# The decays of three batches as exponentials of one scan over logarithms

## The chip, the core and the metric

The kernel runs on one core of a Trainium2 chip. The metric is device time in microseconds (us), the median of three runs. TensorE (PE), VectorE (DVE), ScalarE (ACT), GpSimd (POOL) and SyncE (SP, which issues the transfers) each work through a queue of their own and wait for one another through semaphores.

## What is computed

```python
# B, H, S, D = 4, 8, 768, 48;  f_logit = randn * 0.5 + 2
f = 1.0 / (1.0 + np.exp(-f_logit))
for t in range(S):
    state = f[:, :, t, :, None] * state + np.einsum('bhd,bhe->bhde', k[:, :, t], v[:, :, t])
    y[:, :, t] = np.einsum('bhd,bhde->bhe', q[:, :, t], state)
x = y.transpose(0, 2, 1, 3).reshape(B, S, H * D)
h = x.transpose(0, 2, 1) @ U @ V            # over the sequence, rank 32
u = x + h.transpose(0, 2, 1)
out = u + np.maximum(u @ w_ch1, 0.0) @ w_ch2   # 384 -> 1536 -> 384
```

A gated linear attention and behind it a mixer. The weights U, V, w_ch1 and w_ch2 come in 64 bits and are converted in the kernel.

## The kernel before

**Units and chunks.** The attention is cut into 16 units n: batch b = n // 4 and a pair of its heads, whose channels lie in the two halves of the 128 partitions. The 768 time steps are 12 chunks of C = 64. Inside a chunk a query meets a key by a product q·k (scores, masked to be causal), and between chunks a state of 48 x 48 per head is carried. For that each key is multiplied by X, the product of the gates behind it to the end of its chunk, and each query by Y, the inverse of that product; `least` is the factor of a whole chunk, and `whole` that factor without its first chunk, spread over 48 columns for the scan of the states (L1051). `prepare(n)` holds the steps up to the operands, `attend(n)` those on the operands: `kept` turns the scaled keys `kz` back on TensorE (L1002), `states` makes `ds` (L1026), `scan` adds up the states (L1051, copied to `st` by GpSimd at L1057 in batches 1 and 2), `scores` and `mask` (L975, L988), `read` (L1069) and `inner` (L1087) give y.

**Gates before.** Batch 0 (n < 4) has logarithms of the gates summed by a product on TensorE with a triangle of ones (`log_sums`), and all its factors are exponentials. Batches 1 to 3 work with the gates themselves. `gates` brings raw f to a tile with time along the row and takes its sigmoid into `fz`: units 4 and 5 (n < TURNED = 6) are turned by six transposes on TensorE (L777, `on_tensor`) into one of three PSUM tiles of 4 KB per partition, from unit 6 on VectorE turns them (L754). The raw tiles are `late[:, 0:3]` for even n and `other[:, 0:3]` for odd n. `keep` scans the gates backward into X (L876), copies `least` (L881), and makes `starts` by a maximum and a reciprocal (L883, L884) and `whole` (L886). `keys` multiplies k by X (L802, or L805 behind a transpose). `read` (in the order: read_back) scans the gates forward into Y from `starts` (L894), and `queries` multiplies q by Y.

**The order of work.** TensorE's queue is written by hand in the whole program. VectorE's and ScalarE's are written by hand through batch 0's mixer and the first third of batch 1; behind that a scheduler orders them, and it orders GpSimd throughout. The stretch around units 4 and 5 is this loop (L1286 on), where batch 0's first mixer products run (a tile `pz` of 12 matmuls at L300, emptied by a Relu on ScalarE at L335; two PSUM tiles are shared by `pz`, `pw` and `po`), then a piece of weight conversion is issued, then from the fourth turn on one step of the attention:

```python
second = chain(front(HP, "gates", "keep", "keys", "read_back", "queries"), steps(HP, 2 * HP + 1))
for i, (_, piece) in enumerate(start + m.firsts[1:]):
    piece()
    for f in loads[: 2 if i in (0, 2) else 1]:
        loads.remove(f)
        f()
    if i >= EARLY:
        next(second)()
```

A piece of conversion (`weight_loader`) is two passes on ScalarE (L91, L92), three on VectorE (L98 to L100) and an addition on GpSimd (L101). `w_y` and `w_r` are its tiles. Twelve pieces of w_ch1 are followed by twelve of w_ch2, which the mixer's second product (`po`, L355) reads. Behind the stretch the loop `attention` puts `fill()`, pieces of the mixer of the batch before, between the steps of the units, so that TensorE always has products of the mixer beside those of the attention.

Of the kernel before, what the change touches and what calls it, by code (L numbers as in the profile page):

```python
# [10 lines left out]
F32 = mybir.dt.float32  # L11
# [3 lines left out]
AF = mybir.ActivationFunctionType  # L15
# [549 lines left out]
def factored_path(ctx, tc, q, k, v, f_logit, moe_U, moe_V, moe_w_ch1, moe_w_ch2, out, ok):  # L565
# [135 lines left out]
    for s in range(2):  # L701
        half = causal[s * C : (s + 1) * C, :]
        nc.gpsimd.affine_select(out=half, in_=half, compare_op=ALU.is_ge, fill=0.0, base=0,
                                pattern=[[1, C]], channel_multiplier=-1)
    ends = late[:, 3, :]
    nc.vector.memset(ends, 0.0)
    nc.vector.memset(ends.rearrange("p (c t) -> p c t", t=C)[:, :, C - 1], 1.0)
    starts = other[:, 3, :]
    nc.vector.memset(starts, 0.0)
    fz = [const.tile([P, S + 1], F32, name=f"fz{i}") for i in range(2)]  # L710

    kz = [const.tile([P, C + S], F32, name=f"kz{i}") for i in range(2)]
    for i in range(2):
        nc.gpsimd.memset(kz[i][:, 0:C], 0.0)
    least = const.tile([P, NU, NCH], F32, name="least")

    wholes = [const.tile([P, NCH], F32, name=f"whole{i}") for i in range(2)]
    added = const.tile([P, D * NCH + 1], F32, name="added")
    nc.gpsimd.memset(added[:, 0:1], 0.0)
    for i in range(2):  # L720
        nc.gpsimd.memset(wholes[i][:, 0:1], 0.0)

    U = const.tile([P, NBL, R], F32, name="U")
    V = const.tile([P, (NBL * R + P - 1) // P, P], F32, name="V")
# [22 lines left out]
    def backwards(t, first, n):  # L747

        a = t[:, first : first + 1]
        return bass.AP(a.tensor, a.offset, [list(a.ap[0]), [-1, n]])  # L750

    def turned(t, src_tile):

        nc.vector.transpose(  # L754
            t.rearrange("p (c i) -> p c i", i=NB), src_tile.rearrange("p (c d) -> p c d", d=NB),
        )
# [3 lines left out]
    def prepare(n):  # L760
# [2 lines left out]
        T = units[n] = {}  # L763
        b = n // HP
        r, f = raw[n % 2], fz[n % 2]
        by_chunk = f[:, 0:S].rearrange("p (c t) -> p c t", t=C)

        def follow(nm):

            if n >= HP and n + 2 < NU:  # L770
                load(n + 2, nm)

        def on_tensor(nm):

            pt = ps_big.tile([P, 2, 512], F32, name="pt", tag="big")
            for c in range(NBL):
                nc.tensor.transpose(  # L777
                    pt[:, 2 * c // NBL, c % (NBL // 2) * P : (c % (NBL // 2) + 1) * P],
                    nat[n % 2][nm][:, c].rearrange("p h d -> p (h d)"), ident,
                )  # L780
# [59 lines left out]
        def keep_logs():  # L840
            def blocks_of(t):
                return t.rearrange("p (a c t) -> p a c t", a=2, t=P)

            T["X"], T["Y"] = late[:, 4 + n % 2, :], fz[n % 2][:, 0:S]
            of_least = least[:, n, :].rearrange("p (a c s) -> p a c s", a=2, s=2)
            if n == 0:
                parts = [(slice(a, a + 1), t) for a, t in enumerate(T["sums"])]
            else:
                parts = [(slice(0, 2), T["both"])]
            parts = [(a, t[:, :, 0 : NBL // 2 * (P + 2)].rearrange("p a (c t) -> p a c t", t=P + 2)) for a, t in parts]  # L850
            for a, sums in parts:
                nc.scalar.activation(blocks_of(T["X"])[:, a], sums[:, :, :, 0:P], AF.Exp, scale=-1.0)
            for a, sums in parts:
                nc.scalar.activation(blocks_of(T["Y"])[:, a], sums[:, :, :, 0:P], AF.Exp)
            for a, sums in parts:
                nc.scalar.activation(of_least[:, a], sums[:, :, :, P : P + 2], AF.Exp, scale=-1.0)
            nc.scalar.copy(wholes[n % 2][:, 1:NCH], least[:, n, 1:NCH])

        def gates():
            f0 = T["f0"] = two.tile([P, NCH], F32, name="f0")  # L860
            if n < TURNED:
                pt = on_tensor("f")
                nc.scalar.activation(halves(f)[:, :, :, 1:C], pt[:, :, :, 1:C], AF.Sigmoid)
                nc.scalar.activation(f0.rearrange("p (a c) -> p a c", a=2), pt[:, :, :, 0], AF.Sigmoid)
                follow("f")
                return
            fT = late[:, 6, :]
            turned(fT, r["f"])
            follow("f")
            fv = fT.rearrange("p (c t) -> p c t", t=C)  # L870
            nc.scalar.activation(by_chunk[:, :, 1:C], fv[:, :, 1:C], AF.Sigmoid)  # L871
            nc.scalar.activation(f0, fv[:, :, 0], AF.Sigmoid)

        def keep():
            X = T["X"] = late[:, 4, :]
            nc.vector.tensor_tensor_scan(  # L876
                backwards(X, S - 1, S), backwards(f, S, S), backwards(ends, S - 1, S), 0.0,
                ALU.mult, ALU.add,
            )
            X0 = X.rearrange("p (c t) -> p c t", t=C)[:, :, 0]  # L880
            nc.vector.tensor_copy(least[:, n, :], X0)  # L881
            X1 = two.tile([P, NCH], F32, name="X1")
            nc.vector.tensor_single_scalar(X1, X0, LEAST, ALU.max)  # L883
            nc.vector.reciprocal(starts.rearrange("p (c t) -> p c t", t=C)[:, :, 0], X1)  # L884
            whole = wholes[n % 2]
            nc.vector.tensor_tensor(whole[:, 1:NCH], T["f0"][:, 1:NCH], X0[:, 1:NCH], ALU.mult)  # L886

        def keys():
            operand("k", "X")
# [1 line left out]

        def read():
            Y = T["Y"] = late[:, 5, :]
            nc.vector.tensor_tensor_scan(Y, f[:, 0:S], starts, 0.0, ALU.mult, ALU.add)  # L894

        def queries():
            operand("q", "Y")
# [59 lines left out]
    def attend(n):  # L957
# [50 lines left out]
                spread()  # L1008

        def spread():  # L1010
            whole = T["whole"] = one.tile([P, D, NCH], F32, name="whole")
            nc.scalar.copy(whole, wholes[n % 2].unsqueeze(1).broadcast_to((P, D, NCH)))

        def halves_of(n):
            return [slice(0, D // 2), slice(D // 2, D)] if n == HP - 1 else [slice(0, D)]
# [23 lines left out]
        def scan():  # L1039

            st = T["st"] = two.tile([P, NCH, D], F32, name="st")
            by_e = "p (e c) -> p c e"
            if b == 0:
                states = st.rearrange("p c e -> p (c e)")
                T["st"] = states.rearrange(by_e, c=NCH)
            else:
                states = added[:, 0 : D * NCH]
            with tc.high_priority(offset=2 * AHEAD):
                for e in halves_of(n):
                    of = slice(e.start * NCH, e.stop * NCH)  # L1050
                    nc.vector.tensor_tensor_scan(  # L1051
                        states[:, of], added[:, of], T["whole"].rearrange("p e c -> p (e c)")[:, of], 0.0, ALU.add, ALU.mult
                    )
                if b == B - 1:
                    nc.scalar.copy(st, states.rearrange(by_e, c=NCH))
                elif b:
                    nc.gpsimd.tensor_copy(st, states.rearrange(by_e, c=NCH))  # L1057
# [125 lines left out]
    with tc.manual_schedule(engines={nc.vector.engine, nc.scalar.engine}):  # L1183
# [511 lines left out]
```

## Time and profile before

| what | before |
|---|---|
| three runs | 466.26, 466.35, 466.47 us; median 466.35 |
| the profiled execution: from its first to its last instruction | 463.2 us; the page gives no time for it beside this span |
| TensorE busy | 455.2 us, 98% of the span; granted clock 0.999 |
| VectorE busy | 351.4 us, 76% |
| ScalarE busy | 170.4 us, 37% |
| GpSimd busy | 48.5 us, 10% |

In rows of the order of time the first number is the start in us from the span's start, the second the length; the bracket at the end holds the idle time of the engine before the instruction and what ended it. In groups stand the count, the busy time in us, the mean of one in ns and the idle time before. `out<-in` names the tiles, then come their shapes as partitions x elements. L876 is line 876 of the kernel before. In rows of the compiled order (below) a scan is called SCALAR_TENSOR_TENSOR, and `x6` stands for six equal instructions in a row.

### The profile page before, as it was taken

What the parts mean: (1) busy time and instruction counts of PE and PEld (TensorE: products, weight loads), DVE (VectorE), ACT (ScalarE), POOL (GpSimd) and SP (SyncE); (2) the same over time, 40 slices, a digit from 0 to 9 for tenths busy, and PEclk for the clock granted to TensorE, in tenths of its full rate; (3) what the DMA queues carried; (4) which work ended last, traced back from release to release, by engine and by line L of the source; (5) the groups of instructions that cost most, each with busy time, mean ns of one, the idle gap of its engine ahead of it and who ended that gap; (6) DMA issues with size and microseconds to landing.
All of it is one profiled execution on the core that took longest, in us unless ns stands there. A gap on an engine that the chain in (4) does not pass through costs nothing.

```text
span 463.2 us, 13016 instructions
## 1 busy us (share of the span) xinstructions
PE 455.2 (98%) x5639; PEld 394.5 (85%) x5639; DVE 351.4 (76%) x585; ACT 170.4 (37%) x323; POOL 48.5 (10%) x56
## 2 busy tenths in 40 slices
PE   8999999999999999999999999999999999999997
PEld 5886888875666578999898888899989999999996
DVE  6778788979999677676765559977797887858652
ACT  6785776562333143323322323451412311212200
POOL 2002445634112001010000000000000000000000
PEclk9999999999999999999999999999999999999999
DMA  9959997577777604504633030100000000000001
GB/s 194 186 139 212 227 217 180 150 119 103 124 113 118 107 18 53 78 1 89 77 52 74 14 61 4 28 3 21 18 1 1 35 1 23 13 1 35 1 36 39
DMA packets 148583, 34.35 MB, mean 74 GB/s; under 512 B 136934, under 2 KB 146982, under 8 KB 148518
## 3 DMA queue, kind: packets, MB, share of 16 engines
q1 hardware_dynamic: 147718, 33.29, 37.1%
q8 instruction: 46, 0.75, 0.7%
q10 hardware_dynamic: 800, 0.15, 0.2%
q14 instruction: 19, 0.16, 0.1%
HBM read 28.70 MB, written 4.72 MB: 72 GB/s over the span
## 4 chain that ended last, share of the span: by engine, by line
PE 80%; DVE 11%; ACT 3%; DMA 2%; issue 2%; SPq 2%; DVEq 0%; ACTq 0%
PE pw L389 27%; PE pz L300 21%; PE pp L495 12%; PE po L355 5%; PE y L1069 2%; PE sc L975 2%; PE ds L1026 2%; PE y L1087 2%; PE pt L1002 1%; SPq L661 1%; DVE late L894 1%; PE pt L777 1%; DVE late L876 1%; PE pt L835 1%; DMA other<-in_f_logit_dram 1%
## 5 line engine op out<-in xcount | busy, mean ns | idle before, releaser
L300 PE MATMUL pz<-uT,w 128*128 128x256 f32 x492 | 111.5, 382 | 0.3
L300 PEld LDWEIGHTS pz<-uT,w 128*128 128x128 f32 x492 | 91.7, 190 | 12.9 <-ACT uT L289 0.6
L389 PE MATMUL pw<-zw,w_raw 128*128 128x192 f32 x216 | 38.0, 329 | 0.0
L389 PE MATMUL pw<-w,z_all 128*128 128x192 f32 x216 | 37.3, 327 | 0.0
L335 ACT ACTIVATE z_all<-pz 128x512 f32<-128x512 f32 x33 | 19.6, 598 | 45.1 <-PE pz L300 44.7
L389 PEld LDWEIGHTS pw<-w,z_all 128*128 128x128 f32 x216 | 35.3, 190 | 0.5
L389 PEld LDWEIGHTS pw<-zw,w_raw 128*128 128x128 f32 x216 | 35.1, 190 | 0.6 <-issue 0.3
L101 POOL TENSOR_TENSOR w<-w_y,w_r 128x384 int32<-128x384 int32 x24 | 31.5, 1311 | 37.0 <-DVE w_y L100 22.5
L876 DVE TENSOR_TENSOR_SCAN late<-fz,late 128x768 f32<-128x768 f32 x12 | 21.1, 1755 | 9.4 <-ACT fz L871 9.3
L488 ACT ACTIVATE other<-other 128x512 f32<-128x512 f32 x18 | 11.3, 630 | 40.3 <-DVE other L204 40.3
L355 PE MATMUL po<-w,zw 128*128 128x384 f32 x72 | 25.2, 495 | 0.0
L355 PE MATMUL po<-w,z_all 128*128 128x384 f32 x72 | 24.7, 493 | 0.0
L1057 POOL COPY st<-added 128x576 f32<-128x576 f32 x8 | 12.4, 1556 | 113.8 <-DVE added L1051 113.8
L988 DVE TENSOR_TENSOR A<-sc,causal 128x768 f32<-128x768 f32 x16 | 15.2, 953 | 8.5 <-PE sc L975 8.5
L355 PEld LDWEIGHTS po<-w,zw 128*128 128x128 f32 x72 | 13.2, 190 | 9.6 <-issue 0.8
L894 DVE TENSOR_TENSOR_SCAN late<-fz,other 128x768 f32<-128x768 f32 x12 | 21.0, 1750 | 0.2
L355 PEld LDWEIGHTS po<-w,z_all 128*128 128x128 f32 x72 | 13.3, 190 | 8.9 <-DVE o L204 0.6
L488 ACT ACTIVATE z_all<-z_all 128x512 f32<-128x512 f32 x12 | 7.6, 631 | 34.1 <-DVE z_all L204 34.1
L1034 ACT COPY added<-ds 48x576 f32<-48x576 f32 (+2 forms) x29 | 17.8, 619 | 4.5 <-PE ds L1026 4.1
L495 PE MATMUL pp<-v_nat,late 128*128 128x128 f32 x152 | 19.1, 275 | 0.0
L1069 PEld LDWEIGHTS y<-st,qT 48*64 48x64 f32 x704 | 13.6, 137 | 6.2 <-issue 4.5
L98 DVE TENSOR_SCALAR w_y<-w_y 128x384 f32<-128x384 f32 (+3 forms) x27 | 12.1, 449 | 8.8 <-ACT w_y L91 8.8
(233 smaller groups left out, 872.1 us busy)
## 6 DMA issues: line engine op xcount, KB each, us to landing
w_raw<-in_moe_w_ch_dram SPq DMA_DIRECT2D x18, 384.0 KB, 3.6
out_dram<-o SPq DMA_DIRECT2D x17, 192.0 KB, 1.9
v_nat<-in_v_dram SPq DMA_DIRECT2D x16, 144.0 KB, 3.8
v_nat<-in_v_dram SPq DMA_DIRECT2D x32, 72.0 KB, 3.5
zw<-in_moe_w_ch_dram SPq DMA_DIRECT2D x6, 384.0 KB, 5.1
out_dram<-o SPq DMA_DIRECT2D x14, 96.0 KB, 2.2
w<-in_k_dram SPq DMA_DIRECT2D x4, 288.0 KB, 4.1
w<-in_q_dram SPq DMA_DIRECT2D x4, 288.0 KB, 4.2
```

Source lines behind the costliest of these rows:

```text
L101: nc.gpsimd.tensor_tensor(dst.bitcast(I32), shaped(y.bitcast(I32)), shaped(r), ALU.add)
L300: nc.tensor.matmul(pm[:, i * 2 * P : (i + 1) * 2 * P], lhsT=w1[:, m, o : o + P], rhs=uT[a][:, m, :], start=(m == 0), stop=(m == NDC - 1))
L335: nc.scalar.activation(z[a, c][:, k : k + 2, :].rearrange("p i t -> p (i t)"), pm, AF.Relu)
L355: nc.tensor.matmul(pm, lhsT=z[a, i // NI][:, i % NI, s * P : (s + 1) * P], rhs=w2[:, i, :], start=(i == 0), stop=(i == NFC - 1))
L389: nc.tensor.matmul(W["pm"][:, n * HM : (n + 1) * HM], lhsT=lhs[:, i, :], rhs=rhs[:, i, :], start=(i == 0), stop=(i == NI - 1))
L488: nc.scalar.activation(dst, dst, AF.Relu, scale=float(SIGNS[n]))
L495: nc.tensor.matmul(pm[:, i, r * P : (r + 1) * P], lhsT=room["w"](wn)[:, r * P : (r + 1) * P], rhs=x_node(a, xn), start=((xn, wn) == of[0]) ...
L876: nc.vector.tensor_tensor_scan(backwards(X, S - 1, S), backwards(f, S, S), backwards(ends, S - 1, S), 0.0, ALU.mult, ALU.add,)
L894: nc.vector.tensor_tensor_scan(Y, f[:, 0:S], starts, 0.0, ALU.mult, ALU.add)
L988: nc.vector.tensor_tensor(T["A"], sc[:, :, 0 : NBL * C].rearrange("p h (c i) -> p h c i", i=C), causal.unsqueeze(1).unsqueeze(1).broadcast ...
L1034: nc.scalar.copy(added[r, 1:].rearrange("p (e c s) -> p e c s", c=NBL, s=2)[:, e], ds[r, :, 0 : NBL * D].rearrange("p s (c e) -> p e c s", ...
L1069: nc.tensor.matmul(o(c % 2, par, c // 2), lhsT=T["q"][rows[par], chunk[c]], rhs=T["st"][rows[par], c, :], start=(c <= 2), stop=False, skip ...
```

## The change

Batches 1 to 3 get their factors from logarithms, too, without TensorE's product. `gates` first raises raw f to at least FLOOR = -40 in place, on VectorE for units 4 and 5 and on GpSimd from unit 6 on; then f is turned as before, and ScalarE makes exp(-f) and log(1 + exp(-f)), the negative logarithm of the gate, in `fz`. `keep` is one backward scan of these logarithms, which starts again at each chunk's end (`within` is 1, and 0 there), and behind it two exponentials on ScalarE: X for the first 63 columns of each chunk (the last column of `late[:, 4:6]` is set to 1 once), and `least`. `read` is one more exponential, of the same sums with the other sign, in place of the second scan. The copy, the maximum, the reciprocal and the product for `whole` fall away, and so do the sigmoids with `f0`; `whole` is one tile, filled from `least` directly, which drops a copy in batch 0's `keep_logs` as well. The tiles `ends` and `starts` go, and with them some memsets.

TensorE's queue keeps its 965 rows and their order. On VectorE, at unit 4, behind the ninth piece of weights; `late` holds the raw f of unit 4, X and the constants of the scan, `fz` the gates or their logarithms. Before:

```order
L98 TENSOR_SCALAR w_y<-w_y 128x384
L99 TENSOR_SCALAR w_y<-w_y 128x384
L100 SCALAR_TENSOR_TENSOR w_y<-w_raw,w_y 128x384
L876 SCALAR_TENSOR_TENSOR late<-fz_128,late 128x768
L881 COPY least<-late 128x12
L883 TENSOR_SCALAR X_1141<-late 128x12
L884 RECIPROCAL other<-X_1141 128x12
L886 TENSOR_TENSOR whole_135<-f_1107,late 128x11
```

and now:

```order
L98 TENSOR_SCALAR w_y<-w_y 128x384
L99 TENSOR_SCALAR w_y<-w_y 128x384
L100 SCALAR_TENSOR_TENSOR w_y<-w_raw,w_y 128x384
L859 TENSOR_SCALAR late<-late 128x12x48
L98 TENSOR_SCALAR w_y<-w_y 128x384
L99 TENSOR_SCALAR w_y<-w_y 128x384
L100 SCALAR_TENSOR_TENSOR w_y<-w_raw,w_y 128x384
L869 SCALAR_TENSOR_TENSOR fz_127<-late,fz_127 128x768
```

A new instruction of VectorE, the floor (L859 of the changed kernel), stands behind six pieces of weights and ahead of the seventh, and f's transposes on TensorE (L776 there) now wait for it; the four small steps behind the scan are gone. Unit 5 has the same one behind six more pieces. On GpSimd, around units 6 and 7 (`late` and `other` are their raw f, `w_90` is w_ch2), before:

```order
L101 TENSOR_TENSOR w_89<-w_y,w_r 128x3x128 x12
L101 TENSOR_TENSOR w_90<-w_y,w_r 128x384 x6
L1057 COPY st<-added 128x576
L101 TENSOR_TENSOR w_90<-w_y,w_r 128x384 x6
L1057 COPY st<-added 128x576 x7
```

and now:

```order
L101 TENSOR_TENSOR w_89<-w_y,w_r 128x3x128 x12
L101 TENSOR_TENSOR w_90<-w_y,w_r 128x384 x2
L859 TENSOR_SCALAR late<-late 128x768
L101 TENSOR_TENSOR w_90<-w_y,w_r 128x384 x4
L1044 COPY st<-added 128x576
L101 TENSOR_TENSOR w_90<-w_y,w_r 128x384 x4
L859 TENSOR_SCALAR other<-other 128x768
```

The additions of w_ch2's pieces now have the floors of units 6 and 7 between them. On VectorE around units 7 and 8, in the last third of batch 1 (`other` and `late` are the raw tiles, `o` is a result of the mixer), before:

```order
L884 RECIPROCAL other<-X_1725 128x12
L886 TENSOR_TENSOR whole_136<-f_1715,late 128x11
L754 STREAM_TRANSPOSE kz_131<-other 128x768
L805 TENSOR_TENSOR kz_131<-kz_131,late 128x768
L1051 SCALAR_TENSOR_TENSOR added<-added,whole 128x576
L204 TENSOR_TENSOR o<-x,po 128x384
L988 TENSOR_TENSOR A<-sc,causal 128x768
L894 SCALAR_TENSOR_TENSOR late<-fz_129,other 128x768
L754 STREAM_TRANSPOSE qT<-other 128x768
L805 TENSOR_TENSOR qT<-qT,late 128x768
L754 STREAM_TRANSPOSE late<-late 128x768
L876 SCALAR_TENSOR_TENSOR late<-fz_128,late 128x768
```

and now:

```order
L751 STREAM_TRANSPOSE fz_128<-other 128x768
L869 SCALAR_TENSOR_TENSOR fz_128<-late,fz_128 128x768
L751 STREAM_TRANSPOSE kz_130<-other 128x768
L804 TENSOR_TENSOR kz_130<-kz_130,late 128x768
L1038 SCALAR_TENSOR_TENSOR added<-added,whole 128x576
L204 TENSOR_TENSOR o<-x,po 128x384
L976 TENSOR_TENSOR A<-sc,causal 128x768
L751 STREAM_TRANSPOSE qT<-other 128x768
L804 TENSOR_TENSOR qT<-qT,late 128x768
L751 STREAM_TRANSPOSE fz_127<-late 128x768
L869 SCALAR_TENSOR_TENSOR fz_127<-late,fz_127 128x768
```

The scan of Y (L894) that stood between the mask and the transpose of q is gone, the scan of X (L869 now) writes the sums into `fz`, and the order of the others is kept. ScalarE has, for a unit, exp and log in place of a sigmoid, two exponentials behind the next piece of weights or the next step, and the exponential of Y later; its table load for the sigmoid is gone.

```diff
--- before.py
+++ after.py
@@ -702,23 +702,20 @@
-    ends = late[:, 3, :]
-    nc.vector.memset(ends, 0.0)
-    nc.vector.memset(ends.rearrange("p (c t) -> p c t", t=C)[:, :, C - 1], 1.0)
-    starts = other[:, 3, :]
-    nc.vector.memset(starts, 0.0)
-    fz = [const.tile([P, S + 1], F32, name=f"fz{i}") for i in range(2)]
+    within = late[:, 3, :]
+    nc.vector.memset(within, 1.0)
+    nc.vector.memset(within.rearrange("p (c t) -> p c t", t=C)[:, :, C - 1], 0.0)
+    fz = [const.tile([P, S], F32, name=f"fz{i}") for i in range(2)]
 
     kz = [const.tile([P, C + S], F32, name=f"kz{i}") for i in range(2)]
     for i in range(2):
         nc.gpsimd.memset(kz[i][:, 0:C], 0.0)
     least = const.tile([P, NU, NCH], F32, name="least")
 
-    wholes = [const.tile([P, NCH], F32, name=f"whole{i}") for i in range(2)]
+    whole = const.tile([P, D, NCH], F32, name="whole")
+    nc.gpsimd.memset(whole[:, :, 0], 0.0)
     added = const.tile([P, D * NCH + 1], F32, name="added")
     nc.gpsimd.memset(added[:, 0:1], 0.0)
-    for i in range(2):
-        nc.gpsimd.memset(wholes[i][:, 0:1], 0.0)
 
@@ -763,7 +760,9 @@
         T = units[n] = {}
         r, f = raw[n % 2], fz[n % 2]
-        by_chunk = f[:, 0:S].rearrange("p (c t) -> p c t", t=C)
+
+        def by_chunk(t):
+            return t.rearrange("p (c t) -> p c t", t=C)
...
@@ -854,36 +853,25 @@
                 nc.scalar.activation(blocks_of(T["Y"])[:, a], sums[:, :, :, 0:P], AF.Exp)
             for a, sums in parts:
                 nc.scalar.activation(of_least[:, a], sums[:, :, :, P : P + 2], AF.Exp, scale=-1.0)
-            nc.scalar.copy(wholes[n % 2][:, 1:NCH], least[:, n, 1:NCH])
 
         def gates():
-            f0 = T["f0"] = two.tile([P, NCH], F32, name="f0")
+            raw_f = nat[n % 2]["f"][:, :, :, 0:D] if n < TURNED else r["f"]
+            (nc.vector if n < TURNED else nc.gpsimd).tensor_single_scalar(raw_f, raw_f, FLOOR, ALU.max)
             if n < TURNED:
-                pt = on_tensor("f")
-                nc.scalar.activation(halves(f)[:, :, :, 1:C], pt[:, :, :, 1:C], AF.Sigmoid)
-                nc.scalar.activation(f0.rearrange("p (a c) -> p a c", a=2), pt[:, :, :, 0], AF.Sigmoid)
-                follow("f")
-                return
-            fT = late[:, 6, :]
-            turned(fT, r["f"])
+                nc.scalar.activation(halves(f), on_tensor("f"), AF.Exp, scale=-1.0)
+            else:
+                turned(f, r["f"])
+                nc.scalar.activation(f, f, AF.Exp, scale=-1.0)
             follow("f")
-            fv = fT.rearrange("p (c t) -> p c t", t=C)
-            nc.scalar.activation(by_chunk[:, :, 1:C], fv[:, :, 1:C], AF.Sigmoid)
-            nc.scalar.activation(f0, fv[:, :, 0], AF.Sigmoid)
+            nc.scalar.activation(f, f, AF.Ln, bias=1.0)
 
         def keep():
+            nc.vector.tensor_tensor_scan(
+                backwards(f, S - 1, S), backwards(within, S - 1, S), backwards(f, S - 1, S), 0.0, ALU.mult, ALU.add,
+            )
             X = T["X"] = late[:, 4, :]
-            nc.vector.tensor_tensor_scan(
-                backwards(X, S - 1, S), backwards(f, S, S), backwards(ends, S - 1, S), 0.0,
-                ALU.mult, ALU.add,
-            )
-            X0 = X.rearrange("p (c t) -> p c t", t=C)[:, :, 0]
-            nc.vector.tensor_copy(least[:, n, :], X0)
-            X1 = two.tile([P, NCH], F32, name="X1")
-            nc.vector.tensor_single_scalar(X1, X0, LEAST, ALU.max)
-            nc.vector.reciprocal(starts.rearrange("p (c t) -> p c t", t=C)[:, :, 0], X1)
-            whole = wholes[n % 2]
-            nc.vector.tensor_tensor(whole[:, 1:NCH], T["f0"][:, 1:NCH], X0[:, 1:NCH], ALU.mult)
+            nc.scalar.activation(by_chunk(X)[:, :, 0 : C - 1], by_chunk(f)[:, :, 1:C], AF.Exp, scale=-1.0)
+            nc.scalar.activation(least[:, n, :], by_chunk(f)[:, :, 0], AF.Exp, scale=-1.0)
 
         def keys():
             operand("k", "X")
@@ -891,7 +879,7 @@
 
         def read():
             Y = T["Y"] = late[:, 5, :]
-            nc.vector.tensor_tensor_scan(Y, f[:, 0:S], starts, 0.0, ALU.mult, ALU.add)
+            nc.scalar.activation(by_chunk(Y)[:, :, 0 : C - 1], by_chunk(f)[:, :, 1:C], AF.Exp)
 
         def queries():
             operand("q", "Y")
@@ -1008,8 +996,7 @@
                 spread()
 
         def spread():
-            whole = T["whole"] = one.tile([P, D, NCH], F32, name="whole")
-            nc.scalar.copy(whole, wholes[n % 2].unsqueeze(1).broadcast_to((P, D, NCH)))
+            nc.scalar.copy(whole[:, :, 1:], least[:, n, 1:].unsqueeze(1).broadcast_to((P, D, NCH - 1)))
 
         def halves_of(n):
             return [slice(0, D // 2), slice(D // 2, D)] if n == HP - 1 else [slice(0, D)]
@@ -1049,7 +1036,7 @@
                 for e in halves_of(n):
                     of = slice(e.start * NCH, e.stop * NCH)
                     nc.vector.tensor_tensor_scan(
-                        states[:, of], added[:, of], T["whole"].rearrange("p e c -> p (e c)")[:, of], 0.0, ALU.add, ALU.mult
+                        states[:, of], added[:, of], whole.rearrange("p e c -> p (e c)")[:, of], 0.0, ALU.add, ALU.mult
                     )
@@ -1275,9 +1262,8 @@
-        for t in fz:
-            nc.vector.memset(t[:, 0:S].rearrange("p (c t) -> p c t", t=C)[:, :, 0], 0.0)
-            nc.vector.memset(t[:, S : S + 1], 0.0)
+        for i in range(4, 6):
+            nc.vector.memset(late[:, i, :].rearrange("p (c t) -> p c t", t=C)[:, :, C - 1], 1.0)
```

More of the change, by code (lines that the diff above doesn't have):

```diff
@@ L842, in blocks_of @@
                 return t.rearrange("p (a c t) -> p a c t", a=2, t=P)
-            T["X"], T["Y"] = late[:, 4 + n % 2, :], fz[n % 2][:, 0:S]
+            T["X"], T["Y"] = late[:, 4 + n % 2, :], f
             of_least = least[:, n, :].rearrange("p (a c s) -> p a c s", a=2, s=2)
```

## The prediction

> **What bounds the kernel now.** First the page's shares of the span, then the busy time of each engine by stage (columns: the stretch in us, its length, busy time and instructions of PE, PEld, DVE, ACT and POOL, the granted clock, DMA share, GB/s).
>
> ```profile
> span 463.2 us, 13016 instructions
> PE 455.2 (98%) x5639; PEld 394.5 (85%) x5639; DVE 351.4 (76%) x585; ACT 170.4 (37%) x323; POOL 48.5 (10%) x56
> 47.00:87.00 40.00, 40.00 (x263) 34.87 (x262) 34.70 (x60) 28.29 (x55) 19.59 (x16) 1.00 0.86 199
> 87.00:134.00 47.00, 46.31 (x771) 32.47 (x769) 41.75 (x59) 20.22 (x40) 14.58 (x10) 1.00 0.75 120
> 165.00:315.00 150.00, 149.70 (x2187) 133.71 (x2184) 108.33 (x154) 53.75 (x93) 3.63 (x3) 1.00 0.26 43
> ```
>
> TensorE is never idle in the first of these stages, for 0.69 us in the second, for 0.30 us in the third. Its instructions and their order stay as they are. So all that the change takes from VectorE can give back only what TensorE waits for VectorE, and whatever TensorE newly waits for is paid in full. I looked for both: the waits that end, and the waits that begin.
>
> **The waits that end.** Two gaps in TensorE's order of time stand beside VectorE work of batch 1 (start, length, instruction, idle time before it and its releaser; the transposes of `kz` open a unit's part of TensorE's queue):
>
> ```profile
> 109.85 0.59 PE L1002 MATMUL pt<-ident,kz 64*128 64x64 f32 x12
> 114.86 0.95 DVE L988 TENSOR_TENSOR A<-sc,causal 128x768 f32<-128x768 f32 x1
> 115.91 0.76 PE L1026 MATMUL ds<-v_nat,kb 64*48 64x48 f32 x48 [0.57 <-issue]
> 122.22 0.59 PE L1002 MATMUL pt<-ident,kz 64*128 64x64 f32 x12
> 132.99 0.96 DVE L805 TENSOR_TENSOR kz<-kz,late 128x768 f32<-128x768 f32 x1
> 134.10 0.58 PE L1002 MATMUL pt<-ident,kz 64*128 64x64 f32 x12 [0.21 <-DVE kz L805]
> ```
>
> The `ds` products start 0.10 us after the mask has emptied the scores' PSUM tile (114.86 + 0.95 = 115.81); the profile names no releaser, but the tile pool has three buffers. The first gap is 0.57 us, the second 0.21; the page can count a matmul's modelled end into busy time, so I allow up to 1.1 us for both. What VectorE saves in such a unit: the scan of Y (count, busy us, mean ns), and the four small steps between the scan of X and the transpose of k:
>
> ```profile
> L894 DVE TENSOR_TENSOR_SCAN late<-fz,other 128x768 f32<-128x768 f32 x12 | 21.0, 1750 | 0.2
> 115.72 0.97 DVE L754 STREAM_TRANSPOSE late<-other 128x768 f32<-128x768 f32 x1
> 117.59 1.76 DVE L876 TENSOR_TENSOR_SCAN late<-fz,late 128x768 f32<-128x768 f32 x1 [0.90 <-ACT fz L871]
> 119.85 0.98 DVE L754 STREAM_TRANSPOSE kz<-other 128x768 f32<-128x768 f32 x1
> 127.84 0.97 DVE L754 STREAM_TRANSPOSE late<-late 128x768 f32<-128x768 f32 x1
> ```
>
> A unit takes VectorE 127.84 - 115.72 = 12.1 us, 0.90 of it waiting for the sigmoid. The change takes about 1.7 (Y's scan) and 0.5 (the small steps: at this place the time from 119.35, the end of X's scan, to k's transpose at 119.85) from it, and the wait grows by one more pass of ScalarE, the logarithm (0.7, below): 12.1 - 2.2 + 0.7 = 10.6 us. TensorE's work in such a unit is about 11.6 us (12.4 and 11.9 between the transposes of kz at 109.85, 122.22 and 134.10, less the gaps), so VectorE falls behind it and both gaps close: **-1.1 us** (between -0.8 and -1.1).
>
> **The waits that begin.** Only units 4 and 5 turn f on TensorE, and there the new floor (raw f, maximum with FLOOR) is a VectorE instruction ahead of the transposes. VectorE works in written order in this stage, behind the conversion of weights: six pieces of three instructions (L98 to L100) are issued while TensorE does three tiles of pz. Where the engines stand in time, and the row nearest to the floor:
>
> ```profile
> 47.37 8.04 PE L300 MATMUL pz<-uT,w 128*128 128x256 f32 x36
> 55.24 0.82 PE L777 MATMUL pt<-ident,late 128*128 128x128 f32 x6
> 48.76 0.36 DVE L98 TENSOR_SCALAR w_y<-w_y 128x384 f32<-128x384 f32 x1 [2.18 <-ACT w_y L91]
> 59.31 0.56 DVE L100 SCALAR_TENSOR_TENSOR w_y<-w_raw,w_y 128x384 uint32<-128x384 uint32 x1
> 61.30 0.36 DVE L98 TENSOR_SCALAR w_y<-w_y 128x384 f32<-128x384 f32 x1 [1.44 <-ACT w_y L91]
> 9.51 0.45 DVE L816 TENSOR_SCALAR other<-other 128x576 f32<-128x576 f32 x1
> ```
>
> TensorE reaches f4 at 55.24 and today needs only the load. VectorE, without a break since 48.76, is through the sixth piece at 59.8 (the next instruction starts 0.08 before the printed end). The floor, 576 elements as in batch 0, ends at 59.8 + 0.45 = 60.25, TensorE follows 0.1 later: it waits 60.35 - 55.24 = **5.1 us**. Nothing hides this: the pz products behind f4 stand in the same queue. Bounds: 5.0 to 5.3.
>
> For f5 VectorE is no longer behind by itself, but a loop appears: pz tile, its Relu on ScalarE, behind it the next piece's two ScalarE passes, its three VectorE instructions, the floor, f5's transposes. The loop's steps as they follow each other today:
>
> ```profile
> 79.30 0.82 PE L777 MATMUL pt<-ident,other 128*128 128x128 f32 x6
> 79.50 0.60 ACT L335 ACTIVATE zw<-pz 128x512 f32<-128x512 f32 x1 [1.09 <-PE pz L300]
> 80.00 0.55 ACT L91 ACTIVATE w_y<-w_raw 128x384 f32<-128x384 f32 x1
> 77.99 0.43 DVE L98 TENSOR_SCALAR w_y<-w_y 128x384 f32<-128x384 f32 x1 [0.93 <-ACT w_y L91]
> 79.33 1.75 DVE L876 TENSOR_TENSOR_SCAN late<-fz,late 128x768 f32<-128x768 f32 x1
> ```
>
> TensorE is ready for a transpose at 79.30, the Relu of the tile before starts 0.20 later, the piece's L91 0.50 later, takes 0.55, VectorE's piece 79.33 - 77.99 = 1.34, the floor 0.45, the way back 0.1: 3.15 us from TensorE being ready, however the stage is shifted. VectorE's piece can also be held up by GpSimd, whose new floor of f6 stands between the fourteenth and sixteenth pieces' additions, just there:
>
> ```profile
> 58.22 1.05 DVE L99 TENSOR_SCALAR w_y<-w_y 128x384 uint32<-128x384 uint32 x1
> 58.06 1.00 POOL L101 TENSOR_TENSOR w<-w_y,w_r 128x384 int32<-128x384 int32 x1 [0.95 <-DVE w_y L100]
> 62.80 2.31 POOL L101 TENSOR_TENSOR w<-w_y,w_r 128x384 int32<-128x384 int32 x1 [1.79 <-ACT w_y L91]
> 123.22 1.22 POOL L1057 COPY st<-added 128x576 f32<-128x576 f32 x1 [9.61 <-DVE added L1051]
> ```
>
> L99 takes 1.05 beside an addition of GpSimd instead of 0.36, and the addition 2.31 beside a scan instead of 1.00. GpSimd's floor of 768 elements is in no row; the copy of 576 (1.22) gives 1.6. It costs f5 between nothing and 1.6; I take half, 0.8: **3.9 us** for f5 (3.1 to 4.8). [...]
>
> Two small ones. Behind f4 the Relu of the sixth tile stands behind the exponential of X, which waits for the scan; by the same steps it ends about when tile 8 wants its buffer: 0.1 (0 to 0.5). The last w2 piece already ends late (a 12-matmul row takes 4.41 where the others take 4.14) and is now behind two ScalarE passes of f6 instead of one:
>
> ```profile
> 103.95 4.41 PE L355 MATMUL po<-w,zw 128*128 128x384 f32 x12
> 110.37 4.14 PE L355 MATMUL po<-w,z_all 128*128 128x384 f32 x12
> 105.09 2.31 POOL L101 TENSOR_TENSOR w<-w_y,w_r 128x384 int32<-128x384 int32 x1 [2.72 <-DVE w_y L100]
> ```
>
> 0.3 for it (0 to 0.7, one pass).
>
> **What costs nothing.** ScalarE gets, for one sigmoid pass, Exp, Ln and two more Exp of 768 elements, and loses the table load:
>
> ```profile
> 58.18 1.28 ACT L863 ACT_TABLE_LOAD   x1
> 14.01 0.81 ACT L854 ACTIVATE fz<-pt 128x768 f32<-128x768 f32 x1
> 10.92 0.68 ACT L825 ACTIVATE other<-other 128x576 f32<-128x576 f32 x1
> 145.11 0.96 DVE L805 TENSOR_TENSOR kz<-kz,late 128x768 f32<-128x768 f32 x1
> 171.92 0.58 PE L1002 MATMUL pt<-ident,kz 64*128 64x64 f32 x12
> ```
>
> That is 3 x 0.7 more per unit, 25 us over twelve, on an engine busy 54 of the 150 us of batches 2 and 3. There the operands lie ready long before use (unit 9's kz at 146.07, read at 171.92), so a longer way to them is covered. The table load ends before any product that TensorE waits for. The copies dropped in batch 0 stand before ScalarE's own waits for TensorE: 0. Exponentials in ScalarE's queue in front of Relus in batches 2 and 3: 0.2 (0 to 2, see the second rival).
>
> Sum on the profiled span: 463.2 + 5.1 + 3.9 + 0.1 + 0.3 + 0.2 - 1.1 = 471.7. The median of the runs, 466.35, lies 3.2 above the span (start and end), so **474.9 us**, 1.8% slower.
>
> **The rivals.** (1) The f5 loop is covered: should TensorE's buffers or VectorE's queue put the floor earlier than I read, only f4 is paid: 466.35 + 5.1 - 1.1 + 0.6 = 471.0. For it: a loop of my own working; against it: written order. (2) ScalarE's order couples to VectorE in batches 2 and 3: each exponential waits for a scan of 1.75, a Relu behind it may be late by 2.6 - 0.6 = 2.0 us (a tile's twelve matmuls less the Relu's 0.60) before the tile after next waits. Where VectorE's scan stands behind an addition that waits for TensorE, this decides: 0.4 for each of eight units gives 478. Against it: VectorE idle for 42 of those 150 us. (3) Faster: VectorE's load is what TensorE waits for, and the floors cost nothing, if VectorE at f4 were 5.1 us further on, or TensorE did not wait for them; then the closed gaps remain: 466.35 - 1.1 = 465.2. For it: VectorE is busy 42 of 47 us in batch 1; against it: 48.76 to 59.8 without idle time, on pieces that the change leaves alone. (4) No change within 0.2% (what a measurement of this kernel can tell): gain and f5 loop cancel, f4 not waited for.
>
> **How the numbers follow.** My forecast has 0.70, rivals (1) 0.11, (2) 0.12, (3) 0.04, (4) 0.03. My case's own bounds: 5.0 + 3.1 - 1.1 + 0 = +7.0 to 5.3 + 4.8 - 0.8 + 1.6 = +10.9, so 473.4 to 477.3. The range takes rival (1) in from its middle and part of (2): 471.5 to 477.5. Faster 0.04, same 0.03, slower 0.93.
>
> **What would show it.** A gap of about 5 us on TensorE before f4's transposes, ended by VectorE's floor; one of 3 to 5 before f5's; no gap before `ds` and kz in units 6 to 8; no second table load; TensorE's idle time from unit 6 on no larger than now. If TensorE's gap before f4 is under 3 us, my reading of VectorE's backlog is wrong; if the time lies above 477.5, look at Relus behind exponentials.

## The result, and the profile after

The changed kernel takes **478.50 us** (median of 4 runs, 478.24 to 479.12) where the kernel before takes 466.41 (4 runs, 466.26 to 467.32): ratio 1.0259, 95% interval 1.0240 to 1.0277. It is slower, as forecast, but by 12.1 us where 8.5 were forecast, and the time lies above the range.

The page's shares of the span:

```profile
span 476.8 us, 13025 instructions
PE 458.6 (96%) x5639; PEld 396.9 (83%) x5639; DVE 324.4 (68%) x524; ACT 197.1 (41%) x354; POOL 64.8 (14%) x65
```

and the waits of TensorE (what waits, what ended it, us in total, times, longest):

```profile
PE pt L776 <- DVE late L859: 4.9, 1, 4.9
PE pt L776 <- DVE other L859: 3.2, 1, 3.2
...
PE po L355 <- POOL w L101: 0.8, 1, 0.8
```

VectorE has lost 27 us of work (351.4 to 324.4), ScalarE gained 27, and TensorE waits once for each of the two floors of VectorE. TensorE's instructions are the same 5639 in the same order, so the same instruction can be looked up in both traces, and the difference of its start shows how late the changed kernel is at that place. In what follows f4, k4, f5 and k5 are the transposes of f and k of units 4 and 5. Before, in order of time (the rows at 55.24, 79.30 and 115.91 stand in the prediction):

```profile
37.48 0.75 PE L252 MATMUL ph<-h,blocks 128*128 128x288 f32 x2
61.08 0.82 PE L777 MATMUL pt<-ident,late 128*128 128x128 f32 x6
73.47 0.82 PE L777 MATMUL pt<-ident,other 128*128 128x128 f32 x6
108.29 0.91 PE L1087 MATMUL y<-v_nat,A 64*64 64x48 f32 x48
```

and the changed kernel, with f4 (62.22), k4 (69.67), f5 (85.56), k5 (93.13), and the wait in front of the first products that need the last w_ch2 piece (122.08):

```profile
39.34 0.75 PE L252 MATMUL ph<-h,blocks 128*128 128x288 f32 x2
62.22 1.54 PE L776 MATMUL pt<-ident,late 128*128 128x128 f32 x6 [4.87 <-DVE late L859]
69.67 0.82 PE L776 MATMUL pt<-ident,late 128*128 128x128 f32 x6
85.56 1.25 PE L776 MATMUL pt<-ident,other 128*128 128x128 f32 x6 [3.21 <-DVE other L859]
93.13 0.82 PE L776 MATMUL pt<-ident,other 128*128 128x128 f32 x6
117.78 3.49 PE L355 MATMUL po<-w,zw 128*128 128x384 f32 x10
122.08 0.91 PE L355 MATMUL po<-w,zw 128*128 128x384 f32 x2 [0.82 <-POOL w L101]
122.92 0.92 PE L1074 MATMUL y<-v_nat,A 64*64 64x48 f32 x48
129.70 0.24 PE L1013 MATMUL ds<-v_nat,kb 64*48 64x48 f32 x2
```

| place | before | after | late by | added since |
|---|---|---|---|---|
| end of batch 0's attention | 37.48 | 39.34 | 1.86 | 1.86 |
| f4's transposes | 55.24 | 62.22 | 6.98 | **5.12** |
| k4's transposes | 61.08 | 69.67 | 8.59 | **1.61** |
| f5's transposes | 73.47 | 85.56 | 12.09 | **3.50** |
| k5's transposes | 79.30 | 93.13 | 13.83 | **1.74** |
| behind the last w_ch2 piece | 108.29 | 122.92 | 14.63 | **0.80** |
| `ds` behind the mask | 115.91 | 129.70 | 13.79 | **-0.84** |
| end of the span | 463.2 | 476.8 | 13.6 | -0.2 |

The first row is taken not to be the change's: most of it comes from a wait of 1.36 us in unit 1's `inner` for which the profile names no releaser. Over the profiled executions of this study the shift at that place runs from 0.4 to 2.1 us, and it is 2.1 in the kernel of the second experiment below, whose batch 0 is that of the kernel before. In each run for which both are known the time is 1.7 to 1.9 us above the span (478.54 and 476.8 here), so the profiled execution of before (463.2) was one of about 464.9 us, quicker than its median. Without the first row the table adds up to 11.7 us; the medians differ by 12.1.

The rows that nobody forecast are the two of 1.61 and 1.74 us: TensorE is late by more after each wait has ended. Stretches of the changed kernel, cut where the granted clock changes (columns as before; the clock is the third number from the end):

```profile
55.18:58.60 3.42, 2.17 (x11) 1.56 (x9) 3.28 (x7) 2.60 (x6) 1.55 (x2) 1.00 1.33 197
58.60:62.02 3.42, 0.00 (x0) 0.00 (x0) 3.32 (x6) 1.01 (x3) 1.51 (x3) 1.00 1.03 217
62.02:65.43 3.41, 3.21 (x11) 2.85 (x12) 0.14 (x1) 1.60 (x2) 0.99 (x1) 0.50 1.27 213
65.43:68.84 3.41, 3.41 (x18) 3.00 (x17) 0.46 (x2) 1.56 (x4) 0.00 (x0) 1.00 0.47 131
82.49:85.91 3.42, 0.35 (x3) 0.35 (x4) 1.99 (x4) 1.36 (x3) 2.59 (x3) 1.00 0.56 132
85.91:89.33 3.42, 3.42 (x12) 2.88 (x11) 0.00 (x0) 1.65 (x2) 0.68 (x1) 0.50 0.93 187
89.33:92.74 3.41, 3.41 (x18) 3.00 (x17) 0.86 (x3) 1.49 (x3) 0.00 (x0) 1.00 0.01 2
```

Behind each of the two stretches in which TensorE has done nothing or nearly nothing (0.00 and 0.35 of 3.42 us), it works 3.41 us at a clock of 0.50: the six transposes of f4 take 1.54 us instead of 0.82. Half of 3.41 us is 1.7, which is what the two rows of the table say.

### The profile page after: what moved, and what is told of

It reads as the page before. It is cut to its first block, busy times and chain, and to the rows that moved or that the text cites. A ratio compares the mean times of both kernels' runs of the same rounds, so it can differ in the third digit from the quotient of the medians.

```text
span 476.8 us, 13025 instructions
## 1 busy us (share of the span) xinstructions
PE 458.6 (96%) x5639; PEld 396.9 (83%) x5639; DVE 324.4 (68%) x524; ACT 197.1 (41%) x354; POOL 64.8 (14%) x65
## 4 chain that ended last, share of the span: by engine, by line
PE 87%; DVE 7%; ACT 2%; issue 2%; DMA 1%; POOL 1%; SPq 0%; DVEq 0%; POOLq 0%
PE pw L389 26%; PE pz L300 22%; PE pp L495 12%; PE po L355 9%; PE y L1056 3%; PE sc L963 2%; PE y L1074 2%; PE ds L1013 2%; PE pt L990 2%; PE pt L776 2%; DVE w_y L99 1%; PE pt L834 1%; DVE w_y L100 1%; DMA v_nat<-in_v_dram 1%; PE idle L1177 1%
## 5 line engine op out<-in xcount | busy, mean ns | idle before, releaser
L300 PE MATMUL pz<-uT,w 128*128 128x256 f32 x492 | 114.0, 388 | 0.3
L300 PEld LDWEIGHTS pz<-uT,w 128*128 128x128 f32 x492 | 93.4, 194 | 13.8 <-ACT uT L289 0.6
L101 POOL TENSOR_TENSOR w<-w_y,w_r 128x384 int32<-128x384 int32 x24 | 28.9, 1205 | 47.0 <-DVE w_y L100 24.2
L869 DVE TENSOR_TENSOR_SCAN fz<-late,fz 128x768 f32<-128x768 f32 x12 | 21.1, 1755 | 19.4 <-ACT fz L866 19.3
L1044 POOL COPY st<-added 128x576 f32<-128x576 f32 x8 | 9.8, 1226 | 100.9 <-DVE added L1038 100.9
L204 DVE TENSOR_TENSOR w_raw<-z_all 128x768 f32<-128x768 f32 x12 | 11.4, 951 | 11.7 <-ACT z_all L335 10.3
L1038 DVE TENSOR_TENSOR_SCAN added<-added,whole 128x576 f32<-128x576 f32 x12 | 16.3, 1355 | 4.4 <-ACT added L1021 4.4
L873 ACT ACTIVATE late<-fz 128x756 f32<-128x756 f32 x12 | 10.0, 834 | 22.2 <-DVE fz L869 20.6
```

Of the source, the lines that this page charges most:

```text
L101: nc.gpsimd.tensor_tensor(dst.bitcast(I32), shaped(y.bitcast(I32)), shaped(r), ALU.add)
L300: nc.tensor.matmul(pm[:, i * 2 * P : (i + 1) * 2 * P], lhsT=w1[:, m, o : o + P], rhs=uT[a][:, m, :], start=(m == 0), stop=(m == NDC - 1))
L869: nc.vector.tensor_tensor_scan(backwards(f, S - 1, S), backwards(within, S - 1, S), backwards(f, S - 1, S), 0.0, ALU.mult, ALU.add,)
L1038: nc.vector.tensor_tensor_scan(states[:, of], added[:, of], whole.rearrange("p e c -> p (e c)")[:, of], 0.0, ALU.add, ALU.mult)
```

## The experiments

Theory: all that the change costs is two waits of TensorE for the floors of units 4 and 5, each with a stretch at half clock behind it. Rival: the longer way of the logarithms (three more passes of ScalarE for a unit) costs most of it.

**The change without the two floors.**

```diff
-            (nc.vector if n < TURNED else nc.gpsimd).tensor_single_scalar(raw_f, raw_f, FLOOR, ALU.max)
+            if n >= TURNED:
+                nc.gpsimd.tensor_single_scalar(raw_f, raw_f, FLOOR, ALU.max)
```

> The changed kernel without the floor of units 4 and 5 (it leaves out their maximum with -40, which no input here reaches); all else of the change stays. Theory (TensorE waits for the two floors, and works at half clock behind each wait): the waits of 5.1 and 3.6 us and the slow stretches of 1.5 and 1.65 us go, 478.5 - 11.9 = 466.6 us (466.0 to 467.3), and no granted clock of 0.5 between 55 and 95 us. Rival (the logarithms' longer way to the operands, the added passes of ScalarE, cost most of it): above 472 us.

466.87 us against 466.02 of the kernel before beside it, ratio 1.0017 (1.0004 to 1.0031). The mean granted clock is 1.0. One more of its ten runs took 926.23 us; it is left out of the ratio, and no trace shows why. So the floors of two units of sixteen carry nearly all of the slowdown; the passes of ScalarE do not.

**The floors alone, in the kernel before.**

```diff
             if n < TURNED:
+                raw_f = nat[n % 2]["f"][:, :, :, 0:D]
+                nc.vector.tensor_single_scalar(raw_f, raw_f, FLOOR, ALU.max)
                 pt = on_tensor("f")
```

> The kernel before with nothing added but the floor of units 4 and 5 on VectorE ahead of f's transposes. Theory: the same two waits and slow stretches as in the changed kernel, 466.4 + 5.1 + 1.5 + 3.6 + 1.65 = 478.2 us (476.7 to 478.8; the second wait may be shorter by up to 1.5 since GpSimd has no floors here). Rival (the added passes of ScalarE cost most): 466.4 to 470 us.

477.19 us, ratio 1.0224 (1.0203 to 1.0244). Two instructions of 0.45 us each, in an otherwise unchanged kernel with all the rest of its work on VectorE, cost 11 us. The waits are those of the changed kernel, and the second is shorter by 0.3 without GpSimd's floors:

```profile
PE pt L777 <- DVE late L863: 4.9, 1, 4.9
PE pt L777 <- DVE other L863: 2.9, 1, 2.9
```

**TensorE kept busy in the waits.** The idle products write into the tile that the transposes fill next.

```diff
             pt = ps_big.tile([P, 2, 512], F32, name="pt", tag="big")
+            if nm == "f":
+                for _ in range(20 if n == HP else 11):
+                    nc.tensor.matmul(pt[:, 0, 0:P], lhsT=ident, rhs=ident, start=True, stop=True)
```

> The changed kernel with idle products of TensorE (128x128, 20 ahead of f4's transposes and 11 ahead of f5's) in the time in which it waits for the floors, some 4.2 and 2.4 us of it. Theory (the slow stretches come from TensorE's idleness): the waits' ends stay, the half clock goes, 478.5 - 3.15 = 475.3 us (474.8 to 476.3). Rival (the matmuls behind the waits are slow for another reason, transfers or code that arrive there): 478.5 us or above, and a granted clock of 0.5 as before.

475.09 us: 3.4 us faster than the changed kernel (3.0 when each is taken against the kernel before beside it) by doing 31 products more. f4's part of TensorE's order of time, in which a product stands as two instructions:

```profile
56.79 4.63 PE L777 MATMUL pt<-ident 128*128 128x128 f32 x40
61.83 0.87 PE L779 MATMUL pt<-ident,late 128*128 128x128 f32 x6 [0.42 <-DVE late L862]
```

The transposes take 0.87 us and not 1.54, and the mean granted clock is 1.0 in all four executions, where it is 0.988 to 0.993 in those of the changed kernel. The half clock came from TensorE's idleness. The end of f4's wait did not move: the transposes start 12.92 us behind the start of the row of 36 products ahead of them (48.91), 12.91 in the changed kernel (49.31).

**The waits half filled** (13 and 5 products instead of 20 and 11).

> The changed kernel with fewer idle products (13 and 5) in the two waits, so that TensorE is idle for about 2.1 and 1.9 us at a stretch. If a gap must reach about 3.2 us (the shorter of the two that were followed by half clock), none follows: 475.3 us as with the waits filled. Rival (gaps of 2 us are enough): one or two stretches at a granted clock of 0.5, 476.7 to 478.5 us.

475.84 us. In the profiled execution (475.12 us) gaps of 2.0 and 2.1 us remain, and no stretch at half clock follows:

```profile
58.34:61.76 3.42, 1.74 (x16) 1.54 (x14) 3.32 (x6) 1.13 (x3) 1.53 (x2) 1.00 0.94 210
61.76:65.17 3.41, 3.11 (x18) 2.83 (x19) 0.25 (x1) 1.65 (x2) 1.08 (x1) 1.00 1.27 210
82.22:85.65 3.43, 1.83 (x12) 1.71 (x13) 1.47 (x4) 0.89 (x2) 1.00 (x1) 1.00 0.67 190
85.65:89.07 3.42, 3.42 (x18) 3.01 (x17) 0.64 (x2) 2.25 (x4) 0.00 (x0) 1.00 0.63 104
```

The other three executions (475.82, 477.94 and 475.85 us) have mean granted clocks of 0.996, 0.993 and 0.996. Half clock for 3.41 of some 474 us takes 0.0036 from the mean, so these would be one, two and one such stretches; they have no trace, so where the stretches lay is not shown. By the clock the expectation held in one execution of four, and its rival, that gaps of 2 us are enough, is not ruled out.

**Unit 4's floor two pieces of weights earlier** (four of the six ahead of it). `gates` leaves it out for unit 4, which is not shown here.

```diff
                 loads.remove(f)
                 f()
+                if 24 - len(loads) == 7:
+                    raw_f = nat[HP % 2]["f"][:, :, :, 0:D]
+                    nc.vector.tensor_single_scalar(raw_f, raw_f, FLOOR, ALU.max)
```

> The changed kernel with unit 4's floor written two pieces of weights earlier (behind four of the six), unit 5's as it was. Theory: a piece takes VectorE 1.95 us, so the first wait falls from 5.1 to 1.2 us and no half clock follows it: 478.5 - 3.9 - 1.5 = 473.1 us, up to 474.3 if the Relu behind X's exponential comes to light. Rival (any wait of 1 us is followed by 3.4 us at half clock): 474.6 us or more, and a granted clock of 0.5 behind the first wait.

472.26 us, 6.2 less than the changed kernel and 0.8 less than expected. The first wait is 1.0 us with no half clock behind it; the second, 2.9 where it was 3.2, still has one:

```profile
PE pt L776 <- DVE other L860: 2.9, 1, 2.9
...
PE pt L776 <- DVE late L1280: 1.0, 1, 1.0
```

So the price of the floor is set by its place in VectorE's queue, nearly 2 us for each piece of weights ahead of it (the wait falls from 4.87 to 0.99 us).

**Both floors early.** Unit 4's ahead of the loop, unit 5's in the turn `i == EARLY`, five pieces ahead of its use; `gates` leaves out both, which is not shown.

```diff
+        def floor_of(n):
+            raw_f = nat[n % 2]["f"][:, :, :, 0:D]
+            nc.vector.tensor_single_scalar(raw_f, raw_f, FLOOR, ALU.max)
+        floor_of(HP)
...
+            if i == EARLY:
+                floor_of(HP + 1)
```

> The changed kernel with the floors of units 4 and 5 on VectorE too, but written earlier in its order: unit 4's ahead of the six pieces of weights, unit 5's behind the step that turns unit 4, five pieces ahead of its use. Theory: TensorE waits for neither, 466.6 us as without the floors (466.0 to 467.5). Rival (the floor's own work on VectorE, 0.45 us each in a stage where VectorE has little room, is what costs): 470 us or above.

467.54 us, ratio 1.0036 (1.0021 to 1.0051): just above what was expected (466.0 to 467.5), and some 11 us below the changed kernel with the same instructions. The floors' own work costs next to nothing: 0.67 us more than without the two (466.87). But the kernel is still a little slower than before, with VectorE 27 us lighter, and so is the one without floors. What is left shows on TensorE in both, here in the one without floors:

```profile
62.36 2.75 PE L300 MATMUL pz<-uT,w 128*128 128x256 f32 x12
66.08 2.86 PE L300 MATMUL pz<-uT,w 128*128 128x256 f32 x12 [0.97 <-ACT z_all L335]
```

and on its ScalarE:

```profile
64.60 0.83 ACT L874 ACTIVATE late<-fz 128x756 f32<-128x756 f32 x1 [2.89 <-DVE fz L870]
65.34 0.20 ACT L875 ACTIVATE least<-fz 128x12 f32<-128x12 f32 x1
65.45 0.58 ACT L335 ACTIVATE z_all<-pz 128x512 f32<-128x512 f32 x1
```

ScalarE waits 2.89 us for the scan of unit 4, and a Relu stands behind its two exponentials; TensorE waits for the PSUM tile that this Relu empties. In the changed kernel this was hidden behind the wait for the floor: TensorE does not wait for this Relu there, nor where the waits are filled with products, and it waits 0.26 us for it where the first wait is cut to 1.0 us.

**ScalarE's steps later.** With both floors early, X's exponential and that of `least` move from `keep` to the step after it, behind the next Relu and the next piece; in one of the two kernels the logarithm moves from `gates` to `keep` as well. The lines that these replace are not shown.

```diff
         def keep():
+            nc.scalar.activation(f, f, AF.Ln, bias=1.0)
...
         def keys():
+            if n >= HP:
+                X = T["X"] = late[:, 4, :]
+                nc.scalar.activation(by_chunk(X)[:, :, 0 : C - 1], by_chunk(f)[:, :, 1:C], AF.Exp, scale=-1.0)
+                nc.scalar.activation(least[:, n, :], by_chunk(f)[:, :, 0], AF.Exp, scale=-1.0)
             operand("k", "X")
```

Only the exponentials:

> As the run beside it, but only the exponentials are one step later; the logarithm stays where the changed kernel has it. Theory: the wait for the Relu goes (1.2 to 1.4 us), the one for the last w_ch2 piece (0.8) stays: 467.5 - 1.3 = 466.2 us (465.4 to 466.8). Rival (the Relu is not late because of X's exponential but because of VectorE's pieces): 467.5 us, with the wait at 66 us as it was.

465.97 us against 466.46 of the kernel before beside it, ratio 0.9988 (0.9979 to 0.9996). The wait for the Relu is gone, the one for the last w_ch2 piece (0.8) is still there. With the logarithm too:

> The changed kernel with both floors early, and in batches 1 to 3 the logarithm one step later (in front of the scan) and X's and the chunk's exponentials one step later (in front of the product with k). Theory (without the waits for the floors what is left is a Relu behind X's exponential, 1.4 us, and the last w_ch2 piece behind the logarithm, 0.9 us): 467.5 - 2.0 = 465.5 us (464.7 to 466.3), level with the kernel before or up to 0.4% faster; no wait for the Relu at 66 us, none of 0.8 us for the last piece. Rival (the steps of unit 4 then come too late for those who use them): 467.5 us or above.

**465.18 us**, ratio 0.9973 (0.9963 to 0.9983): 0.3% faster than the kernel before. Of the two waits this is left:

```profile
PE po L355 <- POOL w L101: 0.4, 1, 0.4
```

A kernel before these two made the same moves without the line `if n >= HP`:

> The changed kernel with both floors early as in the run before, and two more moves of ScalarE's work in the written order: the logarithm one step later (in front of the scan, behind the next Relu and the next piece of weights), X's and the chunk's exponentials one step later (in front of the product with k). Theory (what is left of the slowdown without the waits for the floors is a Relu behind X's exponential, 1.4 us, and the last w_ch2 piece behind the logarithm, 0.9 us): 467.5 - 2.0 = 465.5 us (464.7 to 466.2), level with the kernel before or up to 0.3% faster, and TensorE waits neither for the Relu at 66 us nor 0.8 us for the last piece. Rival (the steps of unit 4 are now too late for their users): 467.5 us or above.

There the exponentials ran for batch 0 too and wrote over its own factors. By the program, a smallest `least` below its bound sends the kernel into its general path; in the trace this path starts behind the fast one, at 466 us, and the 1471 us that it all took tell nothing of the question.

## Why the prediction was wrong, step by step

- **TensorE is the bound and what it newly waits for is paid in full**: right. The same 5639 instructions end 13.6 us later, and the table gives each part of it a place.
- **f4's wait, 5.1 us (5.0 to 5.3)**: right, 5.12. VectorE's backlog was read rightly: the sixth piece's last instruction starts at 61.23 and the floor at 61.71, both 1.9 us later than reckoned, which is what batch 0 ended later.
- **f5's wait, 3.9 us (3.1 to 4.8)**: right, 3.50; the loop from the Relu to the floor was there. In the kernel before with the floors alone, the idle time in front of f5 is 2.87 instead of 3.21 us, and so it is with unit 4's floor earlier, where GpSimd's floor runs only behind it (79.91, f5 at 79.14): GpSimd's floor costs 0.3, where 0.8 was put. GpSimd's floor of 768 elements itself takes 2.13 us (estimate: 1.6). VectorE's instructions beside it start later, and only one of them is much longer, 0.66 instead of 0.36 us (the changed kernel, in order of time, both engines):

```profile
83.06 2.13 POOL L859 TENSOR_SCALAR late<-late 128x768 f32<-128x768 f32 x1 [0.43 <-DMA late<-in_k_dram]
83.44 0.66 DVE L98 TENSOR_SCALAR w_y<-w_y 128x384 f32<-128x384 f32 x1 [1.94 <-ACT w_y L91]
84.13 0.36 DVE L99 TENSOR_SCALAR w_y<-w_y 128x384 uint32<-128x384 uint32 x1
84.53 0.56 DVE L100 SCALAR_TENSOR_TENSOR w_y<-w_raw,w_y 128x384 uint32<-128x384 uint32 x1
```

  So the upper end of what the prediction allows for it (0 to 1.6), f5 paying the whole of GpSimd's floor, did not come; the lengths of GpSimd's instructions are rough in a trace, and the 0.3 is read from TensorE's idle time.

- **The step that failed: a wait costs its length.** The sum took the waits at 5.1 and 3.9 us and let TensorE go on behind them at the speed of the row before (0.82 us for six transposes). TensorE was at half clock for 3.41 us behind each: 1.61 and 1.74 us, together 3.35 of the 3.6 us by which the forecast was short. The run with idle products in the waits shows it as the cause: f4's wait ends where it ended, the half clock is gone, and with it 3.0 to 3.4 us. The trace of before shows such a step only at its very end, where it costs nothing: TensorE works 0.83 of 3.42 us, and the granted clock is 0.50 from then on. Ahead of that TensorE is never idle for more than 1.1 us at a time.

```profile
458.89:462.31 3.42, 0.83 (x6) 0.53 (x4) 0.35 (x1) 0.00 (x0) 0.00 (x0) 1.00 0.28 96
462.31:463.16 0.85, 0.00 (x0) 0.00 (x0) 0.00 (x0) 0.00 (x0) 0.00 (x0) 0.50 0.00 0
```

  With half the clock over 3.41 us behind each wait, as the changed kernel's stretches show it, each is 1.7 us dearer (an estimate from these stretches), 474.9 + 2 x 1.7 = 478.3 us in all. Behind 58.60:62.02, in which TensorE did nothing, stand 3.41 us at 0.50; that such a stretch need not be wholly idle is shown below.
- **The last w_ch2 piece, 0.3 us (0 to 0.7)**: the mechanism was right, the size was not: 0.80 us. One pass of ScalarE is 0.84 us there, and nothing else took it up. Moving the logarithm behind the piece brought the wait from 0.8 to 0.4 us.
- **The Relu behind X's exponential, 0.1 us (0 to 0.5)**: not seen in the changed kernel, because the wait for the floor covers it; mis-sized all the same. Once the floors are out of the way TensorE waits 1.0 us for it.
- **The waits that end, -1.1 us (-0.8 to -1.1)**: right, -0.84 in front of `ds` and -0.2 up to the end.
- **ScalarE costs nothing in batches 2 and 3**: right. In the stretch of 152 us that answers to the 150 of before, TensorE is idle for 0.29 us, with ScalarE at 66 us and VectorE at 100:

```profile
178.00:330.00 152.00, 151.71 (x2256) 135.33 (x2255) 99.82 (x132) 66.35 (x109) 12.33 (x7) 1.00 0.26 42
```

- **The rivals.** The second gave 478, next to the measured time, by Relus behind exponentials in batches 2 and 3: the row above shows that it did not happen there, and its number came near by accident. The first (only f4 paid) and the fourth fell with f5's wait. The third (faster, -1.1 us) is the case in which the floors cost nothing; the kernel with both floors early and ScalarE's steps later is that case made by hand, and it is 1.3 us faster than the kernel before.
- **The bounds.** The upper bound of the forecast's own case, 477.3, adds 1.6 us for three small terms whose upper ends are 0.5, 0.7 and 2, together 3.2. With 3.2 it would be 478.9, which takes in the measured 478.5, but that room was meant for waits behind ScalarE, not for the clock.

Still open: what the wait in unit 1's `inner` is for, which differs between executions (none shown before, 1.4 us in the changed kernel); which stretches were at half clock in the three executions without a trace that had the waits half filled; and why in the profiled execution of the kernel with the floors alone (481.43 us, where its other runs took 476.1 to 477.8) the clock was 0.50 from 40.55 to 50.79 us without a long wait ahead of it.

## What to carry to other kernels

A cheap instruction in front of work of the bounding engine cost what was queued ahead of it on its own engine, not what it takes: TensorE waited 4.87 us for a floor of 0.45 us behind six pieces of weights, 0.99 us behind four. So look up where that engine stands at that time, and write the instruction where it is ahead. A wait of TensorE that filled most of one of the 3.41 us windows was dearer by 1.6 to 1.7 us than its length. Idle products that fill the wait gave that back in all four executions; cutting the waits to 2 us did so for certain in only one of four, so 2 us is not to be counted as safe. And when a large wait is removed, look for the small ones that remain or that it covered: here two of about 1 us, both from ScalarE's written order, stood between "no loss" and a gain.

## What the runs showed of the hardware that was not expected

The granted clock changed on a grid: in the traces of before and of the changed kernel each change lies at a whole multiple of 3.413 us from the first record of the clock (134 of them at the end of the program before; 17, 18, 24, 25 and, behind the end, 139 in the changed kernel). In the kernel with the floors alone the stretches at 0.50 (40.55 to 50.79 and 64.44 to 71.27 us) are three and two times 3.41 us long and 13.65 us apart, four times 3.41; the one with unit 4's floor earlier has one of 3.42 us (79.01 to 82.43). Windows of this grid in which TensorE was idle for 80 to 100% were followed by one at 0.50 in each of these cases (the changed kernel twice, 100% and 90%; the kernel with the floors alone, 92%; the one with unit 4's floor earlier, 80%). At the end of the program before it took less, 76% (the rows above). Windows at full clock with 49% idle or less were not (49% and 47% in the stretches shown of the kernel with the waits half filled; 48% and 36% with the floors alone; at most 48% in the changed kernel and 23% in the kernel before), but for the unexplained stretch named above, whose window was idle for 30%; one of 51% that was itself at half clock was followed by another at 0.50. So two waits of the same length were followed by different clocks, by where in the windows they fell. A wait of 2.87 us in the kernel with the floors alone, split over two windows, was followed by full clock:

```profile
84.92:88.33 3.41, 2.19 (x11) 1.58 (x9) 2.19 (x5) 2.85 (x6) 1.93 (x2) 1.00 0.85 167
88.33:91.74 3.41, 1.76 (x11) 1.66 (x12) 1.53 (x4) 1.13 (x3) 1.08 (x1) 1.00 0.77 217
91.74:95.16 3.42, 3.42 (x17) 3.01 (x17) 0.57 (x2) 1.51 (x4) 0.00 (x0) 1.00 0.58 92
```

and one of the same 2.87 us with unit 4's floor earlier, which lay nearly whole in one window, by half clock:

```profile
75.60:79.01 3.41, 0.67 (x4) 0.24 (x2) 1.58 (x4) 1.59 (x4) 1.11 (x2) 1.00 0.94 181
79.01:82.43 3.42, 3.29 (x11) 2.94 (x12) 0.07 (x1) 1.65 (x2) 3.02 (x2) 0.50 0.70 161
```

Between 49% and 76% no window at full clock was read, so from which share of idle time on half clock follows is not shown.
